# Softcap attention, gated MLP and cosine MLP on one core: the background conversion of the second MLP's weights moves beside the first MLP

## The chip, the core and the metric

One core of a Trainium2 chip runs the whole kernel as one program. Its engines run side by side, each through its own queue in order: TensorE (PE, matmuls; PEld its weight loads), VectorE (DVE), ScalarE (ACT), GpSimd (POOL) and SyncE (SP), which issues the DMAs here. They wait for each other by semaphores. The metric is the device time of one execution in microseconds (us).

## What is computed

Inputs are float32 and float64; the weights of the MLPs come as float64 and are converted to float32 on the chip.

```python
scores = cap * tanh((q @ k.T) / sqrt(64) / cap)       # batch 4, heads 12, seq 448, head_dim 64
attn   = softmax(scores) @ v                           # sum + 1e-9 in the denominator
x = attn.transpose(0, 2, 1, 3).reshape(1792, 768)
x = (sigmoid(x @ w_gate) * (x @ w_val)) @ w_out        # d_ff 1536
h = x @ w_in2                                          # d_ff 2048
return (h * cos(h)) @ w_out2                           # 1792 x 768
```

## The kernel before

**Tiles and halves.** The 1792 tokens are worked in two halves of 896 (two batches of 448). A float32 product is made of three matmuls: each operand is split into a rounded part and a rest, and `mm3` (L496) adds rest x rounded and rounded x rest to rounded x rounded. A tile of weights, a *unit*, is 128 x 768 (some 128 x 512).

**Order of the stages.** Attention of half 0; the first MLP of half 0 with pieces of the attention of half 1 between; attention of half 1; the first MLP of half 1; the second MLP of half 1; the second MLP of half 0. The result y of the first MLP on half 0 waits in DRAM (`ykept`) and is fetched and split again by `y_again` (L579) in the last group of the second MLP of half 1; the tiles are then `yr` (fetched) and `ya` (split).

**First MLP** (`mlp1`, L514). Twelve rounds m: 36 matmuls of the gate (`pg`), 36 of the value (`pv`). ACT makes the sigmoid of `pg` (L545) beside `pv`, DVE multiplies (L547), ACT and DVE split the product (L549, L550). Then six y rounds of 72 matmuls (`py`); ACT copies y out of PSUM (L574), DVE makes its rest (L575). `pg`, `pv`, `py` and later `ph` take turns in the two buffers of one PSUM pool (`psS`, L93), so the next `pg` needs the sigmoid of this one, and `py` of round m+2 the y copy of round m.

**Second MLP** (`mlp2`, L594). f-groups of 6, 5 and 5 tiles. Per f tile 36 matmuls `ph` (L500), then a chain of ACT and DVE for h cos h (`hidden`, L659), with a split that gives z; then the products `po` of the group (L619), which ACT copies or DVE adds into `acc`.

**Weights.** A unit that is there in float32 is fetched from DRAM (`f<-kept`, L140), rounded by ACT (L224), and its rest is made by POOL (L225). Three are fetched ahead; the tiles f have four slots (`FB`, L64), shared with the background's tiles `fb`.

**Background** (`background`, L196). The second MLP's weights, 34 units, are converted in three steps each, in program order between other work; each `next(others)` is one step:

```python
        for _ in signs(raw[u], g):            # step 1: ACT: Abs (L156) into fb, Sign (L158)
        ...                                   #         and the DMA of the next raw unit
        next(c); next(c)                      # step 2: DVE L163, L165
        for _ in c: pass                      # step 3: DVE L169, L173
        nc.sync.dma_start(out=kept[u][:, : nk * n], in_=g)   # write-back, L214
```

One further step in front loads the first raw unit: 103 steps. Before, 4 steps follow each of the twelve gate/value rounds (`PIECES`), 4 lie in each y round (`BESIDE_Y`), 2 follow each `hidden` of the second MLP of half 1 (`PIECES_H`), and some lie between its products (`BESIDE_O`).

The order on each engine is the order of the program (`manual_schedule`, L715): nothing is moved ahead of what was written first.

Of the kernel before, what the change touches and what calls it, by code (L numbers as in the profile page):

```python
# [27 lines left out]
def softcap_attention_gated_mlp_cos_mlp(  # L28
# [18 lines left out]
    nc = tc.nc  # L47
# [6 lines left out]
    KD, KF, KF2 = DM // P, DFF // P, DFF2 // P  # L54
    BH = 2
    TOK = BH * S
    NTT = TOK // P
# [11 lines left out]
    BESIDE = ((2, 10), (3, 2), (3, 6), (4, 1), (4, 5), (4, 8), (5, 1), (5, 5), (5, 8))  # L69

    PIECES, BESIDE_Y, PIECES_H, BESIDE_O = 4, (2, 5, 8, 11), 2, (4, 8, 12, 16, 20)

    AGAIN = (4, 6, 8, 10, 12, 14, 16)


    PVS = ((), (), (0, 1, 2, 3), ())
# [17 lines left out]
    def big_tile(shape, dtype, name):  # L96
        return big.tile(shape, dtype, tag="big", name=name)
# [27 lines left out]
    ykept = [dram.tile([P, BH, S], F32, tag=f"ykept{i}", name=f"ykept{i}") for i in range(KD)]  # L125
# [126 lines left out]
    def w_early():  # L252

        for _ in w_signs():
            pass

    def w_front(mid=nothing):

        if pos["conv"] == len(units):
            mid()  # L260
            return
        if pos["sign"] == pos["conv"]:
            w_early()
        for i, _ in enumerate(w_conv()):
            if i == 1:
                mid()
        w_loads()
# [6 lines left out]
    def w_back():  # L274
        if pos["split"] < len(units):
            if pos["keep"] == pos["split"]:
                w_keep()
            w_split()
            w_loads()
# [22 lines left out]
    def w_take():  # L302
        i = pos["use"]
        pos["use"] += 1
        return w_t.pop(i)
# [205 lines left out]
    def tmp_tile(name):  # L511
        return tmp.tile([P, BH, S], F32, tag="tmp", name=name)
# [66 lines left out]
    def y_again(y):  # L579

        raw = {}
        for m in range(-1, KD):
            if m + 1 < KD:
                raw[m + 1] = tmp_tile(f"yr{m + 1}")
                nc.sync.dma_start(out=raw[m + 1], in_=ykept[m + 1])
            if m >= 0:
                t = raw.pop(m)
                yt = big_tile([P, 2, BH, S], F32R, f"ya_{m}")
                nc.scalar.copy(out=yt[:, 0], in_=t)
                nc.vector.tensor_tensor(out=yt[:, 1], in0=t, in1=yt[:, 0].bitcast(F32), op=ALU.subtract)  # L590
                y.append(yt)
            yield

    def mlp2(hf, y, others, beside):  # L594
        acc = {}
        for gi, (f0, nf) in enumerate(groups):
            last = gi == len(groups) - 1
            z = []
            for f in range(f0, f0 + nf):
                t, more = hidden(hf, f, y, f0 + nf - 1 - f)  # L600
                z.append(t)
                for _ in range(PIECES_H):
                    next(others, None)
            zf = [t.rearrange("p a c s -> p a (c s)") for t in z]
            for nb in range(DM // NB):
                ws = [w_take() for _ in range(0, nf, UK)]
                pos_t = {}

                def out_tile(t, name):
                    if nb == 0 and t == EARLY - 1:  # L610
                        return more[:, 0]
                    return psA.tile([P, 512], F32, tag="A", name=name)

                def product(t, kks):
                    for kk in kks:
                        if kk == 0:
                            pos_t[t] = out_tile(t, f"po{hf}_{gi}_{nb}_{t}")
                        for zi, wi in ((0, 0), (0, 1), (1, 0)):
                            nc.tensor.matmul(  # L619
                                pos_t[t][:, :NB],  # L620
                                lhsT=zf[kk][:, zi, t * P : (t + 1) * P],
                                rhs=ws[kk // UK][:, wi, kk % UK, :],
                                start=(kk == 0 and (zi, wi) == (0, 0)),
                                stop=(kk == nf - 1 and (zi, wi) == (1, 0)),
                            )


                early = range(EARLY if nb == 0 else 0)
                for t in range(NTT):
                    if t == 0:  # L630
                        for e in early:
                            product(e, range(nf - 2))
                        for e in early:
                            product(e, range(nf - 2, nf - 1))
                    product(t, range(nf - 1 if t in early else 0, nf))
                    ps = pos_t.pop(t)
                    if gi == 0:
                        if t == 0:
                            acc[nb] = big_tile([P, NTT, NB], F32, f"acc{hf}_{nb}")
                        nc.scalar.copy(out=acc[nb][:, t], in_=ps[:, :NB])  # L640
                    else:
                        a = acc[nb][:, t]
                        nc.vector.tensor_tensor(out=a, in0=ps[:, :NB], in1=a, op=ALU.add)
                    if t == 2:
                        w_back()
                    if t in ((0, 2, 4) if nb == 0 else (0, 3)):
                        w_early()
                    if t in ((2, 4, 6) if nb == 0 else (2, 5)):
                        w_front()
                    if t == NTT - 1:  # L650
                        w_back()
                    if last:
                        store(hf, t, nb, acc[nb][:, t])
                        if nb * NTT + t in AGAIN:
                            next(beside, None)
                    elif nb * NTT + t in BESIDE_O:
                        next(others, None)

    def hidden(hf, f, y, left):  # L659

        w = w_take()
        ps = ps_tile(f"ph{hf}_{f}")
        more = ps_tile(f"more{hf}_{f}") if left == 0 else None
        for kk in range(KD):
            mm3(ps, w, kk, y[kk], kk == 0, kk == KD - 1)

        h = tmp_tile(f"h{hf}_{f}")
        u = tmp_tile(f"u{hf}_{f}")
        n = tmp_tile(f"n{hf}_{f}")
        zt = big_tile([P, 2, BH, S], F32R, f"z{hf}_{f}")  # L670

        def fraction(c):
            nc.scalar.activation(out=u[:, c], in_=ps[:, c, :S], func=AF.Identity, scale=INV_TWO_PI, bias=quarter)  # L673
            nc.vector.tensor_scalar_add(out=n[:, c], in0=u[:, c], scalar1=ROUND)  # L674
            nc.vector.scalar_tensor_tensor(
                out=u[:, c], in0=n[:, c], scalar=ROUND, in1=u[:, c], op0=ALU.subtract, op1=ALU.subtract
            )

        def product(c, h):
            nc.scalar.activation(out=u[:, c], in_=u[:, c], func=AF.Sin, scale=-TWO_PI_LOW)  # L680
            nc.vector.tensor_tensor(out=n[:, c], in0=h, in1=u[:, c], op=ALU.mult)

        def split(c, engine):
            nc.scalar.copy(out=zt[:, 0, c], in_=n[:, c])
            engine.tensor_tensor(out=zt[:, 1, c], in0=n[:, c], in1=zt[:, 0, c].bitcast(F32), op=ALU.subtract)

        both = slice(0, BH)
        if left == 0:
            for c in range(BH):
                fraction(c)  # L690
            for c in range(BH):
                product(c, ps[:, c, :S])
                split(c, nc.vector)
            w_back()
        else:
            nc.scalar.copy(out=h, in_=ps[:, :, :S])
            fraction(both)
            w_step(lambda: product(both, h))
            split(both, nc.vector if left == 1 else nc.gpsimd)
        return zt, more  # L700
# [14 lines left out]
    with tc.manual_schedule():  # L715
        nc.vector.memset(zeros, 0.0)
        nc.vector.reciprocal(out=tanh_scale, in_=cap_sb)
        nc.vector.tensor_scalar_mul(out=tanh_scale, in0=tanh_scale, scalar1=1.0 / float(D) ** 0.5)
        nc.scalar.activation(out=guard, in_=cap_sb, func=AF.Exp, scale=-1.0)
        nc.vector.tensor_scalar_mul(out=guard, in0=guard, scalar1=1e-9 / CP)  # L720
        att = [attention(hf) for hf in range(B // BH)]
        steps = 3 + (BH * NP + 1) * NC - LAST
        for _ in range(steps):
            next(att[0])
        mlp1(0, att[0], att[1])
        for _ in range(steps - len(BESIDE)):
            next(att[1])
        others = background()
        y = mlp1(1, att[1], others)
        y_first = []  # L730
        mlp2(1, y, others, y_again(y_first))
        mlp2(0, y_first, iter(()), iter(()))


# [33 lines left out]
```

## Time and profile before

| | |
|---|---|
| median of 3 runs | 1275.12 us (1274.87 to 1278.29) |
| profiled execution | 1271.98 us, span 1270.2 us, mean granted clock 0.985 |
| busy share of the span | PE 96%, PEld 83%, DVE 55%, ACT 47%, POOL 35% |
| the chain that ended last | PE 72%, DVE 13%, ACT 6%, issue 4%, DMA 3% |

The chain is followed back from the last instruction to what released each step. Times in timelines are us from the start of the span; a figure in brackets is the time that the engine stood idle before the row, and what released it. `x36` is the number of instructions merged in a row.

### The profile page before, as it was taken

The page shows a single profiled execution, that of the slowest core. Times are in us where ns is not written, and L with a number is a line of the kernel's source. Part 1 is how long each engine was busy: PE and PEld are TensorE (multiplying, and loading weights), DVE is VectorE, ACT ScalarE, POOL GpSimd, SP SyncE. Part 2 cuts the span into 40 slices and gives each one's busy share as a digit, 9 for nine tenths or more (in the row PEclk, how much of TensorE's full clock was granted, in tenths as well). Part 3 has the DMA queues.
Part 4 walks back from the last instruction along what each step waited for, and adds up shares of the span by engine and source line. Part 5 has one row for each costly group of instructions (what it writes and reads, how often), then busy time and mean ns, then how long its engine had stood idle before and what let it go on. Part 6 is the DMA issues. An engine that isn't in the chain of part 4 may idle for free.

```text
span 1270.2 us, 17272 instructions
## 1 busy us (share of the span) xinstructions
PE 1220.0 (96%) x7014; PEld 1051.7 (83%) x7014; DVE 696.4 (55%) x757; ACT 593.5 (47%) x678; POOL 449.9 (35%) x234
## 2 busy tenths in 40 slices
PE   8989999999999999999999997699699999999998
PEld 4445889999985558899999996699599999999998
DVE  6998797778516983455445445514543435024252
ACT  7885654445337892433343335435414335344150
POOL 3766232233216672232223233223233234335041
PEclk9999999999999999999999999899799999999999
DMA  6422465446633313455455523332231441213012
GB/s 154 138 72 87 150 211 188 160 150 223 189 108 99 88 30 102 131 165 173 147 168 163 182 87 100 112 104 83 91 104 34 138 146 50 63 42 97 8 47 83
DMA packets 131376, 148.26 MB, mean 117 GB/s; under 512 B 50529, under 2 KB 101345, under 8 KB 131297
## 3 DMA queue, kind: packets, MB, share of 16 engines
q1 hardware_dynamic: 131008, 147.09, 38.0%
q8 instruction: 55, 0.90, 0.3%
q14 instruction: 25, 0.20, 0.1%
q10 hardware_dynamic: 288, 0.07, 0.0%
HBM read 112.13 MB, written 35.00 MB: 116 GB/s over the span
## 4 chain that ended last, share of the span: by engine, by line
PE 72%; DVE 13%; ACT 6%; issue 4%; DMA 3%; POOL 1%; SPq 1%; DVEq 0%; ACTq 0%; POOLq 0%
PE po L619 16%; PE ph L500 13%; PE py L500 12%; PE pv L500 11%; PE pg L500 10%; PE pv L408 4%; PE s L379 3%; DMA kept<-fb 2%; DVE r L427 1%; PE t L358 1%; DVE fb L169 1%; DVE fb L173 1%; ACT p L382 1%; DVE f L169 1%; PE den L424 1%
## 5 line engine op out<-in xcount | busy, mean ns | idle before, releaser
L225 POOL TENSOR_TENSOR w<-f,w 128x768 fp32r<-128x768 f32 (+1 forms) x140 | 271.3, 1943 | 704.0 <-ACT w L224 572.9
L619 PE MATMUL po<-w,z 128*128 128x256 f32 x1920 | 243.3, 288 | 21.6 <-ACT w L224 7.8
L619 PEld LDWEIGHTS po<-w,z 128*128 128x128 f32 x1920 | 239.0, 196 | 24.6 <-ACT w L224 8.0
L500 PE MATMUL pv<-x,w 128*128 128x448 f32 x864 | 180.7, 366 | 1.2 <-DVE sg L547 1.2
L500 PE MATMUL pg<-x,w 128*128 128x448 f32 x864 | 180.8, 367 | 0.1
L500 PE MATMUL py<-g,w 128*128 128x448 f32 x864 | 179.1, 367 | 0.5 <-ACT sg L545 0.5
L500 PEld LDWEIGHTS pv<-x,w 128*128 128x128 f32 x864 | 161.9, 188 | 17.0 <-issue 3.3
L500 PEld LDWEIGHTS pg<-x,w 128*128 128x128 f32 x864 | 161.8, 188 | 16.2 <-ACT sg L545 1.1
L500 PEld LDWEIGHTS py<-g,w 128*128 128x128 f32 x864 | 161.5, 188 | 16.1 <-issue 1.0
L500 PE MATMUL ph<-y,w 128*128 128x448 f32 x576 | 121.0, 372 | 7.4 <-ACT u L673 7.4
L224 ACT CAST w<-f 128x768 fp32r<-128x768 f32 (+1 forms) x140 | 111.8, 808 | 30.1 <-DVE f L173 16.2
L500 PEld LDWEIGHTS ph<-y,w 128*128 128x128 f32 x576 | 110.2, 192 | 17.4 <-ACT u L673 8.2
L674 DVE TENSOR_SCALAR n<-u 128x896 f32<-128x896 f32 (+1 forms) x38 | 26.2, 690 | 172.5 <-ACT u L673 172.5
L500 PE MATMUL ph<-ya,w 128*128 128x448 f32 x576 | 117.2, 365 | 0.0
L500 PEld LDWEIGHTS ph<-ya,w 128*128 128x128 f32 x576 | 108.0, 188 | 8.5
L382 ACT ACTIVATE p<-s,tanh_scale 112x896 f32<-112x896 f32 x96 | 93.1, 1011 | 43.3 <-PE s L379 43.2
L388 ACT ACTIVATE p<-p,cap_sb 112x1792 f32<-112x1792 f32 x48 | 86.4, 1799 | 0.1
L379 PEld LDWEIGHTS s<-st 64*112 64x112 f32 x576 | 46.4, 174 | 41.0 <-ACT p L382 19.0
L408 PE MATMUL pv<-p,v 112*64 112x448 f32 x384 | 77.5, 545 | 2.0 <-PE t L358 2.0
L379 PE MATMUL s<-st 64*112 64x448 f32 x576 | 74.4, 385 | 1.6 <-ACT p L382 1.4
L427 DVE RECIPROCAL r<-den 128x448 f32<-128x448 f32 x24 | 70.8, 2950 | 8.6 <-PE den L424 8.6
L163 DVE TENSOR_SCALAR fb<-fb 128x768 f32<-128x768 f32 (+1 forms) x34 | 30.0, 882 | 82.6 <-ACT fb L156 82.6
(82 smaller groups left out, 1237.9 us busy)
## 6 DMA issues: line engine op xcount, KB each, us to landing
f<-kept SPq DMA_DIRECT2D x92, 384.0 KB, 3.1
kept<-f SPq DMA_DIRECT2D x36, 384.0 KB, 2.7
wi_raw<-in_moe_w_in_dram SPq DMA_DIRECT2D x16, 768.0 KB, 5.1
kept<-fb SPq DMA_DIRECT2D x28, 384.0 KB, 2.7
wg_raw<-in_moe_w_gate_dram SPq DMA_DIRECT2D x12, 768.0 KB, 5.1
wv_raw<-in_moe_w_val_dram SPq DMA_DIRECT2D x12, 768.0 KB, 4.7
wo_raw<-in_moe_w_out_dram SPq DMA_DIRECT2D x12, 768.0 KB, 4.8
wz_raw<-in_moe_w_out_dram SPq DMA_DIRECT2D x12, 768.0 KB, 4.9
```

Of the source, the lines that this page charges most:

```text
L163: nc.vector.tensor_scalar(out=g, in0=g, scalar1=F64_MIN_HI, scalar2=F64_MAX_HI, op0=ALU.max, op1=ALU.min)
L169: nc.vector.scalar_tensor_tensor(out=gi, in0=lo, scalar=28, in1=gi, op0=ALU.logical_shift_right, op1=ALU.bitwise_or)
L224: nc.scalar.copy(out=t[:, 0], in_=r)
L225: nc.gpsimd.tensor_tensor(out=t[:, 1], in0=r, in1=t[:, 0].bitcast(F32), op=ALU.subtract)
L379: nc.tensor.matmul(ps[:CP, h, :S], lhsT=st[r, ki, ks], rhs=st[r, qi], start=(n == 0), stop=(n == 2))
L382: nc.scalar.activation(out=pt[:CP, j], in_=ps[:CP, :, :S], func=AF.Tanh, scale=tanh_scale[:CP])
L388: nc.scalar.activation(out=pt[:CP], in_=pt[:CP], func=AF.Exp, scale=cap_sb[:CP])
L408: nc.tensor.matmul(pv[h * D : (h + 1) * D, :S], lhsT=tv[:, h, c, :], rhs=pt[:CP, j, h, :], start=(c == 0), stop=(c == NC - 1),)
L427: nc.vector.reciprocal(out=r[:, 0], in_=den[:, :S])
L500: nc.tensor.matmul(ps[:, c, :S], lhsT=w[:, wi, kk, :], rhs=x[:, xi, c, :], start=(first and (wi, xi) == (0, 0)), stop=(last and (wi, xi) = ...
L619: nc.tensor.matmul(pos_t[t][:, :NB], lhsT=zf[kk][:, zi, t * P : (t + 1) * P], rhs=ws[kk // UK][:, wi, kk % UK, :], start=(kk == 0 and (zi, ...
L674: nc.vector.tensor_scalar_add(out=n[:, c], in0=u[:, c], scalar1=ROUND)
```

## The change

The steps of the background lie beside the first MLP of half 1 alone: 5 behind each gate/value round, 7 in each y round; what is left is issued behind the y rounds. The second MLP no longer has steps of it. `y_again` issues a fetch two of its steps ahead of the conversion, before one, and begins at product 2 instead of 4.

```diff
-    PIECES, BESIDE_Y, PIECES_H, BESIDE_O = 4, (2, 5, 8, 11), 2, (4, 8, 12, 16, 20)
-
-    AGAIN = (4, 6, 8, 10, 12, 14, 16)
+    PIECES, BESIDE_Y = 5, (0, 2, 4, 6, 8, 9, 11)
+
+    AGAIN = (2, 4, 6, 8, 10, 12, 14, 16)
@@ def y_again(y):
-        for m in range(-1, KD):
-            if m + 1 < KD:
-                raw[m + 1] = tmp_tile(f"yr{m + 1}")
-                nc.sync.dma_start(out=raw[m + 1], in_=ykept[m + 1])
+        for m in range(-2, KD):
+            if m + 2 < KD:
+                raw[m + 2] = tmp_tile(f"yr{m + 2}")
+                nc.sync.dma_start(out=raw[m + 2], in_=ykept[m + 2])
@@ def mlp2(hf, y, beside):
                 z.append(t)
-                for _ in range(PIECES_H):
-                    next(others, None)
...
                         if nb * NTT + t in AGAIN:
                             next(beside, None)
-                    elif nb * NTT + t in BESIDE_O:
-                        next(others, None)
@@ main
         y = mlp1(1, att[1], others)
         y_first = []
-        mlp2(1, y, others, y_again(y_first))
-        mlp2(0, y_first, iter(()), iter(()))
+        for _ in others:
+            pass
+        mlp2(1, y, y_again(y_first))
+        mlp2(0, y_first, iter(()))
```

The lines of the changed kernel have numbers one less than before up to the last part (L155 is L156, L223 is L224).

ACT's order before, gate/value round 3 of half 1: from the split of its product (`g_3`) to the sigmoid of round 4 (`sg_4`); `fb` is a unit of the background.

```order
L549 CAST g_3_4408<-sg_3_4363 128x896
L224 CAST w_4411<-f_4266 128x768
L156 ACTIVATE fb_4419<-wi_raw 128x768
L158 ACTIVATE wi_raw<-wi_raw,tiny 128x768
L545 ACTIVATE sg_4_4466<-pg_4_4429 128x896
```

The same place in the changed kernel:

```order
L548 CAST g_3_4418<-sg_3_4373 128x896
L223 CAST w_4421<-f_4271 128x768
L155 ACTIVATE fb_4429<-wi_raw 128x768
L157 ACTIVATE wi_raw<-wi_raw,tiny 128x768
L155 ACTIVATE fb_4439<-wz_0_0_raw 128x768
L157 ACTIVATE wz_0_0_raw<-wz_0_0_raw,tiny 128x768
L544 ACTIVATE sg_4_4481<-pg_4_4444 128x896
```

A second Abs and its Sign stand ahead of the sigmoid of round 4.

ACT's order before, from the last y rounds into the second MLP of half 1 (`h_0`, `u_0` belong to its first f tile):

```order
L224 CAST w_5746<-f_5602 128x768
L574 CAST y_4_5751<-py_4_5653 128x896
L224 CAST w_5796<-f_5648 128x768
L156 ACTIVATE fb_5819<-wi_raw 128x768
L158 ACTIVATE wi_raw<-wi_raw,tiny 128x768
L224 CAST w_5844<-f_5700 128x768
L574 CAST y_5_5849<-py_5_5754 128x896
L696 COPY h_0_5889<-ph_0_5852 128x896
L673 ACTIVATE u_0_5890<-ph_0_5852,quarter 128x896
...
L684 CAST z_0_5892<-n_0_5891 128x896
L156 ACTIVATE fb_5909<-wi_raw 128x768
L158 ACTIVATE wi_raw<-wi_raw,tiny 128x768
```

The same place in the changed kernel:

```order
L573 CAST y_4_5841<-py_4_5733 128x896
L155 ACTIVATE fb_5880<-wz_2_0_raw 128x768
L157 ACTIVATE wz_2_0_raw<-wz_2_0_raw,tiny 128x768
L223 CAST w_5891<-f_5728 128x768
L155 ACTIVATE fb_5925<-wz_2_3_raw 128x512
L157 ACTIVATE wz_2_3_raw<-wz_2_3_raw,tiny 128x512
L223 CAST w_5942<-f_5783 128x768
L573 CAST y_5_5947<-py_5_5844 128x896
L691 COPY h_0_5990<-ph_0_5953 128x896
L668 ACTIVATE u_0_5991<-ph_0_5953,quarter 128x896
...
L679 CAST z_0_5993<-n_0_5992 128x896
L691 COPY h_1_6044<-ph_1_6007 128x896
```

The Abs of the 34th and last unit now stands ahead of the copy of y_5; no Abs follows in the second MLP.

## Rows read from the trace of the kernel before

**Rows 1.** By stretch: length, busy (xcount) PE PEld DVE ACT POOL, clock, DMA share, GB/s.

```profile
743.80:858.30 114.50, 96.18 (x595) 90.69 (x594) 50.55 (x47) 47.73 (x69) 31.45 (x15) 0.93 0.30 95
858.30:951.50 93.20, 80.30 (x498) 76.19 (x497) 46.02 (x61) 34.49 (x45) 28.93 (x15) 0.91 0.30 95
951.50:1028.30 76.80, 75.35 (x498) 71.86 (x497) 30.71 (x46) 31.26 (x39) 24.68 (x14) 1.00 0.36 107
1028.30:1117.50 89.20, 89.20 (x596) 85.90 (x595) 23.01 (x28) 37.06 (x57) 31.08 (x16) 1.00 0.23 66
1117.50:1191.80 74.30, 74.30 (x497) 71.63 (x496) 25.96 (x41) 27.01 (x35) 27.42 (x15) 1.00 0.19 57
1191.80:1266.30 74.50, 74.45 (x497) 71.57 (x495) 26.34 (x43) 23.41 (x30) 20.11 (x11) 1.00 0.19 53
```

**Rows 2.** Timeline of ACT, second MLP of half 1: start, length, instruction, idle before.

```profile
765.38 0.90 ACT L156 ACTIVATE fb<-wi_raw 128x768 f32<-128x768 f32 x1 [7.23 <-DMA kept<-fb]
...
767.18 0.89 ACT L696 COPY h<-ph 128x896 f32<-128x896 f32 x1
```

**Rows 3.** Timeline of PE, from the y rounds into the second MLP.

```profile
654.58 89.40 PE L500 MATMUL py<-g,w 128*128 128x448 f32 x432 [0.50 <-ACT sg L545]
743.82 22.48 PE L500 MATMUL ph<-y,w 128*128 128x448 f32 x108
769.03 14.86 PE L500 MATMUL ph<-y,w 128*128 128x448 f32 x72 [2.73 <-ACT u L673]
788.55 10.32 PE L500 MATMUL ph<-y,w 128*128 128x448 f32 x36 [4.66 <-ACT u L673]
```

**Rows 4.** Timeline of ACT, y rounds of the first MLP.

```profile
665.74 0.89 ACT L156 ACTIVATE fb<-wi_raw 128x768 f32<-128x768 f32 x1 [8.38 <-DMA kept<-fb]
...
672.74 0.90 ACT L156 ACTIVATE fb<-wi_raw 128x768 f32<-128x768 f32 x1 [5.06 <-DMA kept<-fb]
...
674.60 1.56 ACT L224 CAST w<-f 128x768 fp32r<-128x768 f32 x2
...
738.56 0.91 ACT L156 ACTIVATE fb<-wi_raw 128x768 f32<-128x768 f32 x1 [6.34 <-DMA kept<-fb]
```

**Rows 5.** Timeline of SP's queue: two write-backs of the background, issued.

```profile
594.60 0.32 SPq L214 DMA_DIRECT2D kept<-fb  x1
...
669.91 0.32 SPq L214 DMA_DIRECT2D kept<-fb  x1
```

**Rows 6.** Timeline of DVE, y rounds.

```profile
668.92 0.96 DVE L173 SCALAR_TENSOR_TENSOR fb<-fb,wi_raw 128x768 int32<-128x768 int32 x1
...
675.93 2.42 DVE L173 SCALAR_TENSOR_TENSOR fb<-fb,wi_raw 128x768 int32<-128x768 int32 x1
678.27 1.08 DVE L575 TENSOR_TENSOR y<-py,y 128x896 fp32r<-128x896 f32 x1
```

**Rows 7.** Chain of waits, last group of the second MLP, half 1.

```profile
1004.68 4.81 DMA yr<-ykept
```

**Rows 8.** Timeline of ACT, gate/value rounds.

```profile
590.43 0.90 ACT L156 ACTIVATE fb<-wz_raw 128x768 f32<-128x768 f32 x1 [6.73 <-DMA kept<-fb]
...
607.25 0.91 ACT L156 ACTIVATE fb<-wz_raw 128x768 f32<-128x768 f32 x1 [4.89 <-DMA kept<-fb]
...
609.08 0.91 ACT L545 ACTIVATE sg<-pg 128x896 f32<-128x896 f32 x1
```

**Rows 9.** Timeline of PE, gate/value rounds.

```profile
573.33 7.46 PE L500 MATMUL pv<-x,w 128*128 128x448 f32 x36
580.62 7.46 PE L500 MATMUL pg<-x,w 128*128 128x448 f32 x36
```

**Rows 10.** Busy time by stretch, behind the wait at 788.55; columns as in rows 1.

```profile
788.50:792.00 3.50, 3.45 (x9) 3.10 (x10) 2.42 (x3) 1.67 (x2) 0.00 (x0) 0.50 0.00 0
796.00:800.00 4.00, 3.95 (x24) 3.54 (x22) 1.70 (x1) 0.00 (x0) 0.88 (x1) 1.00 0.48 152
```

**Rows 11.** Costliest groups of the page: busy us, mean ns of one, idle before.

```profile
L225 POOL TENSOR_TENSOR w<-f,w 128x768 fp32r<-128x768 f32 (+1 forms) x140 | 271.3, 1943 | 704.0 <-ACT w L224 572.9
```

More of the change, by code (lines that the diff above doesn't have):

```diff
@@ L592, in y_again, with mlp2 @@
             yield
-    def mlp2(hf, y, others, beside):
+    def mlp2(hf, y, beside):
         acc = {}
```

## The prediction

> **What bounds the kernel now.** I read the table of stages first, then the timelines of PE, ACT, SP and DVE at the places the change touches. TensorE bounds the kernel: it is busy nearly throughout, except in two stretches [rows 1]. These are the first two f-groups of the second MLP on the second half of the tokens (743.8 to 951.5). The same code on the first half, later, takes 89.2 and 74.3 us with PE busy throughout; here it takes 114.5 and 93.2 us, with the granted clock at 0.93 and 0.91. The code differs in one thing: here the background conversion runs in between. What it does is seen on ACT [rows 2]: an Abs (L156) of the background waits 7.23 us for the write-back of the unit before it, and the copy of `ph` (L696), whose matmuls were over, comes only behind it. PE then waits, 4.66 us before one group of 36 matmuls [rows 3].
>
> So the background has a chain of its own: Abs on ACT, four operations on DVE, the write-back `kept`, and only then the next Abs, because the f loads hold the other three f slots. One unit alone takes 7.0 us, from 665.74 to 672.74 [rows 4]. Its write-back is issued at 669.91 [rows 5] and lands 2.8 us later. Over nine Abs, 665.74 to 738.56, the eight intervals mean 9.1 us [rows 4]. Between them lie eleven weight copies (L224), the first two at 674.60 [rows 4], each followed by a subtraction on POOL (L225). With one of these beside it the last DVE operation takes 2.42 instead of 0.96 us [rows 6]; f loads, y copies and y subtractions come between as well. Beside the first MLP this chain runs as it does in the second; but there PSUM's two buffers give ACT time, and PE hardly waits.
>
> **The change part by part.** The amount of conversion stays: 34 units, 103 steps. Before, 72 steps lay beside the first MLP and 31, some ten units, beside the second; now 60 lie in its twelve gate/value rounds (5 per round, before 4), 42 in the six y rounds (7, before 4), and the last is issued right behind them.
>
> *Removed from the second MLP.* The second half then runs the code that the first half runs. I take the first half's times: 114.5 + 93.2 - 89.2 - 74.3 = 44.2 us gained [rows 1], clock included. Of that little can be missing, since nothing else differs in those two groups. Lower bound: if only the ten Abs's own waits went but the other stalls stayed, perhaps half, 22.
>
> *Fetching y two steps ahead.* It adds no DMA. The six loads of 448 KB are issued one of its steps earlier, two output tiles, and so pass the stores of two tiles on SP's queue; the conversions stay where they were. In the last group the chain of waits goes twice through a `yr` load, the first time 4.81 us [rows 7]. The group takes 76.8 us against 74.5 for the first half's [rows 1]. At most 2.3 us go, at worst none; I take 2.0. What hides the earlier loads are the products of two more tiles; without that cover the 2.0 stay.
>
> *Gate/value rounds, 5 steps.* Let E be the end of `pv` of a round. Call a unit's steps s (Abs and Sign), a and b (the halves on DVE, b with the write-back). Of three rounds in a row the first reads s a b s a, the second b s a b s, the third a b s a b. The first kind is in the profile already, less its last a: second Abs at 607.25, sigmoid at 609.08, done at 609.98 [rows 8]; PE's next `pg` needs that buffer 14.6 us after E (two times 7.29, [rows 9]), so it just holds. The second kind was there only without its last s. There E is 580.79 [rows 9], the Abs starts at 590.43 [rows 8], its write-back is issued at 594.60 [rows 5], 13.8 behind E. The added Abs stands in ACT's order ahead of the next sigmoid: 13.8 + 2.8 landing + 2.73 (from that Abs's start to the sigmoid's end, 607.25 to 609.98) = 19.4 us behind E. PE waits 19.4 - 14.6 = 4.8 us. The third kind then catches up: its write-back lands before PE needs it. Such rounds are the rounds 3, 6 and 9 of 0 to 11: 3 x 4.8 = 14.4 us. Queued behind the waiting Abs are the sigmoid, the weight copy (L224) and with it POOL's subtraction; PE waits for the sigmoid first.
>
> *The clock.* After the 4.66 us wait the granted clock was 0.50, that is 1.2 of 2.4 GHz, and 1.00 again in the stretch from 796 [rows 10]; the 36 matmuls took 10.32 instead of 7.46 us [rows 3, 9]: 2.9 us. A wait of 4.8 us should do the same: 3 x 2.9 = 8.7. Bounds: 0 if the clock holds, 8.7.
>
> *The y rounds, 7 steps.* Steps run ahead of PE, since no step waits for it, so the background goes at its chain's pace, not PE's. PE gives 89.2 us for six rounds (654.58 to 743.82, [rows 3]); 14 units at 9.1 would need 127. My value for a unit: bare 7.0, the measured mean 9.1 with 11 weight copies on 8 intervals (1.4 a unit); now 12 on 14 (0.86), so 7.0 + 2.1 x 0.86/1.4 = 8.25 us, 14 x 8.25 = 115.5. The round before y is of the first kind, so its second Abs stands 11.8 us behind E (607.25 - 595.4, E one round of 14.6 behind 580.79). The last Abs is then at E + 127.3. Then come on ACT this Abs and its Sign (some 0.7 each at 512 columns, the 0.90 of [rows 4] scaled), a weight copy (0.78, half of the two of [rows 4]) and the copy of y_5 (0.89, as `ph`'s of the same size in [rows 2]), then y_5's subtraction on DVE (1.08, [rows 6]) and the last four matmuls of `ph` 0 (0.8), together 5.0 us: E + 132.3. Before, `ph` 0 ended at 743.82 + 7.46 = 751.3 and E was 654.58 - 0.50 = 654.1 [rows 3], so 97.2. Loss 35.1 us. What waits: `py` for the weight copy and the y copy that stand behind an Abs, in small pieces, then `ph` 0 for w, y_4 and y_5. One more loss of clock, 2.9, behind the longest wait; those inside the y rounds cost nothing, since ACT is later than PE there. Bounds for the loss: 14 units at 7.0 give 17.6, at 9.1 they give 47.
>
> A rule speaks against this size. The row shows that one collision with POOL costs DVE 1.46 us (2.42 - 0.96), and a subtraction takes 1.94 us on average [rows 11]. The Trainium skill, "SBUF — State Buffer", section "SBUF: two separate sides", says that DVE and GpSimd lock their shared port pair exclusively, for a whole instruction. By that rule a DVE operation that comes just behind a subtraction's start waits for nearly all of it. My 8.25 us hold 17.5 us of collisions and the like (14 x 1.25); a whole subtraction for each of the 12 copies would be 23.3.
>
> *Sum.* 14.4 + 8.7 + 35.1 + 2.9 = 61.1 lost, 44.2 + 2.0 = 46.2 gained: 14.9 us slower. The profiled execution took 1271.98 us (span 1270.2), so 1286.9; the median of the three runs, 1275.12, lies 3.1 above it, so I predict 1290.
>
> **The rivals.**
> *The other side: the chain is quick.* If nothing collides in the y rounds and the units of 512 columns, 4 of the 14, are shorter (by a third in the operations, so some 5.4 us by estimate), they take 10 x 7.0 + 4 x 5.4 = 91.6 instead of 115.5: 9.0 us faster than before, 1266. It decides at 8.25 - 14.9/14 = 7.2 us a unit. For it: the first of the eight intervals is 7.0. Against it: their mean. Chance 0.12.
> *The clock holds*, because the waits come out a little shorter than 4.66: 11.6 less, 3.3 slower, 1278. For it: behind a wait of 2.73 us 72 matmuls took 14.86 us, full speed [rows 3]. Chance 0.13.
> *Every collision costs the most it can.* A whole subtraction for each of the 12 copies makes 14 x 7.0 + 23.3 = 121.3, 5.8 more, 1296; units that stay at the mean of 9.1 make 127.4, 11.9 more, 1302. For it: the mean of the eight intervals, and more traffic than before. Against it: fewer copies per unit. Chance 0.17.
> *The second MLP keeps half of its stalls*: 22 less gained, 1312. Against it: the first half's time. Chance 0.03.
>
> **How the numbers follow.** My forecast has 0.55; its own range is 1281 to 1298. About 0.3%, 3.8 us, is what this measurement can tell. Faster by more: nearly all of the first rival, 0.11. Within: most of the second and little of the rest, 0.11. Slower: 0.78. The range of 1270 to 1304 leaves out most of the first rival and all of the fourth, 0.13, and little of the rest.
>
> **What would show it.** Right: the two groups from the first `ph` on take 89 and 74 us at clock 1.00; three gaps of nearly 5 us ahead of `pg` in rounds 5, 8 and 11, released by the sigmoid, with slow matmuls behind; the y rounds and `ph` 0 take some 35 us more, with `ph` 0 held by y_5, and ACT's idle time there ended by `kept`. Wrong: Abs intervals below 7.2 us in the y rounds, or a first sigmoid gap that is missing; then the whole is faster. If gaps remain in the second MLP, the gain was not the background's.

## The result and the profile after

The changed kernel takes 1290.54 us (median of 4 runs, 1288.03 to 1291.71) against 1274.99 (1270.05 to 1278.29) for the kernel before: ratio 1.0134, 95% interval 1.01 to 1.0168. It is 15.5 us slower; predicted were 14.9 us, and a time of 1290. Its profiled execution has a span of 1288.6 us, 18.4 more than before. Followed along PE, the difference comes from these stretches (us):

| stretch | before | after | difference | predicted |
|---|---|---|---|---|
| start to the first `pg` of half 1 (472.24, 475.79) | 472.2 | 475.8 | +3.6 | 0 |
| gate/value rounds of half 1, to the first `py` | 182.3 | 205.0 | +22.6 | +23.1 |
| y rounds and `ph` 0, to ACT's copy of `ph` 0 | 96.9 | 134.2 | +37.4 | +35.1 |
| rest of f-groups 1 and 2 | 200.0 | 157.6 | -42.5 | -44.2 + 2.9 |
| f-group 3 | 76.8 | 74.3 | -2.5 | -2.0 |
| half 0 of the second MLP and the end | 241.9 | 241.7 | -0.2 | 0 |

The first line is no work of the change: the code there is the same (the last section comes back to it). Without it the rows sum to 14.8.

The table of stages of the changed kernel; columns as in [rows 1].

```profile
680.80:813.60 132.80, 105.22 (x466) 94.05 (x465) 63.05 (x71) 42.79 (x52) 25.30 (x14) 0.89 0.50 159
813.60:898.30 84.70, 84.70 (x563) 81.66 (x563) 21.64 (x26) 38.45 (x58) 29.52 (x15) 0.97 0.21 65
898.30:972.60 74.30, 74.30 (x498) 71.62 (x497) 25.90 (x41) 27.02 (x35) 27.37 (x15) 1.00 0.20 57
972.60:1046.90 74.30, 74.30 (x498) 71.62 (x497) 31.73 (x48) 31.26 (x39) 26.34 (x14) 1.00 0.38 113
```

Two things are to be seen. Behind `ph` 0 PE is busy throughout the second MLP now: where [rows 1] had 93.2 and 76.8 us there are 74.3 twice. And the y rounds with `ph` 0, in which PE hardly waited before, now leave it idle for 27.6 us (132.80 - 105.22). What PE waited for from the first MLP of half 1 on: us in total, times, longest.

```profile
PE pg L499 <- ACT sg L544: 17.4, 6, 5.1
PE py L499 <- DVE y L574: 14.8, 4, 5.4
PE ph L499 <- ACT y L573: 10.4, 1, 10.4
PE ph L499 <- DVE y L574: 2.4, 1, 2.4
```

The longest two of the kernel before, over the same stretch, were these:

```profile
PE po L619 <- ACT w L224: 7.8, 1, 7.8
PE ph L500 <- ACT u L673: 7.4, 2, 4.7
```

Both lay in the second MLP and are gone, like its smaller ones; what stands in the list now is the sigmoid's and the y copies'. PE's timeline has them at the places that were forecast; the rows answer to [rows 3] and [rows 9].

```profile
511.74 7.56 PE L499 MATMUL pg<-x,w 128*128 128x448 f32 x36 [1.84 <-ACT sg L544]
...
561.60 9.50 PE L499 MATMUL pg<-x,w 128*128 128x448 f32 x36 [5.06 <-ACT sg L544]
...
612.86 9.57 PE L499 MATMUL pg<-x,w 128*128 128x448 f32 x36 [4.86 <-ACT sg L544]
...
664.52 9.13 PE L499 MATMUL pg<-x,w 128*128 128x448 f32 x36 [4.98 <-ACT sg L544]
673.48 7.46 PE L499 MATMUL pv<-x,w 128*128 128x448 f32 x36
680.77 29.35 PE L499 MATMUL py<-g,w 128*128 128x448 f32 x144
...
795.11 6.46 PE L499 MATMUL ph<-y,w 128*128 128x448 f32 x30 [2.35 <-DVE y L574]
811.99 41.11 PE L499 MATMUL ph<-y,w 128*128 128x448 f32 x186 [10.42 <-ACT y L573]
```

The three gaps of 4.9 to 5.1 us stand ahead of `pg` of rounds 5, 8 and 11, and the 36 matmuls behind each take 9.1 to 9.6 us. `ph` 0 stops after 30 of 36 matmuls and waits 10.42 us for the copy of y_5.

ACT shows why. Round 3 of the gate/value rounds, which answers to [rows 8]: two Abs, the second behind a write-back, and only then the sigmoid, done at 561.55, just before PE starts at 561.60.

```profile
551.98 0.89 ACT L155 ACTIVATE fb<-wi_raw 128x768 f32<-128x768 f32 x1 [7.52 <-issue]
...
558.85 0.89 ACT L155 ACTIVATE fb<-wz_raw 128x768 f32<-128x768 f32 x1 [4.93 <-DMA kept<-fb]
...
560.65 0.90 ACT L544 ACTIVATE sg<-pg 128x896 f32<-128x896 f32 x1
```

And in the y rounds, which answer to [rows 4], ACT does little and waits for write-backs to the end; the copy of y_5 (L573) comes behind the last Abs.

```profile
685.98 0.66 ACT L155 ACTIVATE fb<-wz_raw 128x512 f32<-128x512 f32 x1 [2.13 <-POOL w L224]
...
691.39 0.89 ACT L155 ACTIVATE fb<-wz_raw 128x768 f32<-128x768 f32 x1 [3.94 <-DMA kept<-fb]
...
808.97 0.66 ACT L155 ACTIVATE fb<-wz_raw 128x512 f32<-128x512 f32 x1 [6.64 <-DMA kept<-fb]
...
811.04 0.90 ACT L573 CAST y<-py 128x896 fp32r<-128x896 f32 x1
```

From the Abs at 691.39 to the one at 808.97 are 14 units in 117.6 us, 8.40 each.

### The profile page after: what moved, and what is told of

It is laid out like the page before. It is cut to its first block, busy times and chain, and to the rows that moved or that the text cites. A ratio compares the mean times of both kernels' runs of the same rounds, so it can differ in the third digit from the quotient of the medians.

```text
span 1288.6 us, 17313 instructions
## 1 busy us (share of the span) xinstructions
PE 1226.7 (95%) x7014; PEld 1055.2 (82%) x7014; DVE 681.4 (53%) x757; ACT 595.1 (46%) x678; POOL 446.4 (35%) x234
## 4 chain that ended last, share of the span: by engine, by line
PE 66%; DVE 14%; ACT 6%; issue 6%; DMA 5%; POOL 2%; SPq 0%; ACTq 0%; DVEq 0%; POOLq 0%
PE ph L499 18%; PE po L616 18%; PE py L499 7%; PE pv L499 7%; PE pg L499 7%; DMA kept<-fb 5%; PE pv L407 3%; PE s L378 3%; DVE fb L172 3%; DVE fb L168 2%; ACT fb L155 2%; DVE r L426 1%; PE t L357 1%; ACT p L381 1%; DVE f L168 1%
## 5 line engine op out<-in xcount | busy, mean ns | idle before, releaser
L224 POOL TENSOR_TENSOR w<-f,w 128x768 fp32r<-128x768 f32 (+1 forms) x140 | 270.3, 1935 | 725.9 <-ACT w L223 647.4
L616 PE MATMUL po<-w,z 128*128 128x256 f32 x1920 | 234.4, 283 | 0.0
L616 PEld LDWEIGHTS po<-w,z 128*128 128x128 f32 x1920 | 232.6, 192 | 0.3
L499 PE MATMUL pg<-x,w 128*128 128x448 f32 x864 | 187.6, 376 | 17.4 <-ACT sg L544 17.4
L499 PE MATMUL py<-g,w 128*128 128x448 f32 x864 | 187.9, 379 | 14.8 <-DVE y L574 14.8
L499 PEld LDWEIGHTS pg<-x,w 128*128 128x128 f32 x864 | 166.1, 193 | 36.8 <-ACT sg L544 19.9
L499 PEld LDWEIGHTS py<-g,w 128*128 128x128 f32 x864 | 168.2, 196 | 32.2 <-DVE y L574 16.3
L223 ACT CAST w<-f 128x768 fp32r<-128x768 f32 (+1 forms) x140 | 112.0, 808 | 29.1 <-DVE f L172 16.1
L162 DVE TENSOR_SCALAR fb<-fb 128x768 f32<-128x768 f32 (+1 forms) x34 | 24.8, 728 | 102.2 <-ACT fb L155 102.2
```

Of the source, the lines that this page charges most:

```text
L223: nc.scalar.copy(out=t[:, 0], in_=r)
L224: nc.gpsimd.tensor_tensor(out=t[:, 1], in0=r, in1=t[:, 0].bitcast(F32), op=ALU.subtract)
L499: nc.tensor.matmul(ps[:, c, :S], lhsT=w[:, wi, kk, :], rhs=x[:, xi, c, :], start=(first and (wi, xi) == (0, 0)), stop=(last and (wi, xi) = ...
L616: nc.tensor.matmul(pos_t[t][:, :NB], lhsT=zf[kk][:, zi, t * P : (t + 1) * P], rhs=ws[kk // UK][:, wi, kk % UK, :], start=(kk == 0 and (zi, ...
```

## The experiments

Theory A is the prediction's: the background is a chain through one tile slot (the next Abs waits until the write-back of the last unit has landed), and since ACT works in order, what stands behind a waiting Abs is late. Theory B, the rival: the loss is the price of so much conversion beside the first MLP, its share of DVE, of the port with POOL and of the DMA engines, whatever the order or the slot.

**The same steps, three Abs moved behind a sigmoid.**

```diff
-                for _ in range(PIECES):
+                for _ in range(PIECES - (m in (3, 6, 9))):
                     next(beside, None)
@@ behind the sigmoid and w_step() of the gate part
+                        if hf and m in (4, 7, 10):
+                            next(beside, None)
```

> The changed kernel, but the fifth step of gate/value rounds 3, 6 and 9 of half 1 (an Abs and its Sign) is issued behind the next round's sigmoid instead of ahead of it. Same steps, same slot, same traffic. Theory A (the Abs that waits for a write-back stands ahead of the sigmoid): the three gaps of 4.9 us and the slow matmuls behind them (some 2.0 us each) go, 20.7 us, to about 1270; the y rounds stay as they are. Theory B (the loss is the amount of conversion, port and DMA traffic beside the first MLP): no change, about 1290.

Measured: 1273.85 us (median of 10), 1.0006 of the kernel before (0.9993 to 1.002), 16.7 us less than the changed kernel. (The two ran beside different runs of the kernel before; each taken against its own, 1272.89 here and 1274.99 there, the gain is 14.6.) What PE waited for:

```profile
PE py L499 <- DVE y L576: 15.5, 4, 5.6
PE ph L499 <- ACT y L575: 8.8, 1, 8.8
PE pg L499 <- ACT sg L544: 6.3, 5, 2.1
```

The waits for the sigmoid fall from 17.4 to 6.3 us, the longest from 5.1 to 2.1; those of the y rounds stay. The work is the same, so theory B has no account of it. The gain is 4 us or more short of the forecast: the trace has smaller gaps, of 0.7 to 1.3 us, ahead of four other rounds, and behind the one of 2.06 us ahead of round 2 the 36 matmuls take 9.16 us.

**The same steps, slots of their own.**

```diff
-            g = f_tile(f"b{u}")[:, : nk * n]
+            g = tmp.tile([P, UW], F32, tag="tmp", name=f"b{u}")[:, : nk * n]
```

> The changed kernel, but the background's tiles come from the pool of temporary tiles (four slots, one of them taken by the sigmoid's tile) instead of sharing the four f slots. Same steps at the same places, same bytes. Theory A (a chain through one slot: the next Abs waits until the write-back has landed): an Abs waits for its raw unit only, ACT keeps up, the gaps ahead of pg and in the y rounds go: 36 us of the y rounds and ph 0, 17 us of waits and some 6 of clock in the gate/value rounds, together up to 58, to about 1233. Theory B (amount of conversion and traffic beside the first MLP): at most a few us, 1285 or more.

Measured: 1226.18 us (median of 4, 1225.16 to 1230.29), 0.9632 of the kernel before (0.9604 to 0.9661): this version beats both kernels, by 48.8 us (46.7 against the kernel before on its own chip) and by 64.4. That is 6 us more than was expected; half of these are in the y rounds and `ph` 0, which give back 39 us and not 36. From the first MLP of half 1 on, PE waited for one thing only:

```profile
PE pg L499 <- ACT sg L544: 1.2, 3, 0.6
```

The stages, the y rounds first, then f-groups 1 and 2; columns as in [rows 1].

```profile
654.00:745.00 91.00, 91.00 (x451) 84.34 (x450) 64.48 (x71) 41.24 (x50) 23.46 (x13) 1.00 0.71 234
745.40:834.70 89.30, 89.30 (x596) 85.98 (x595) 24.20 (x27) 39.60 (x60) 31.32 (x16) 1.00 0.21 65
834.70:909.00 74.30, 74.30 (x497) 71.63 (x497) 25.89 (x41) 27.02 (x35) 27.41 (x15) 1.00 0.19 57
```

The same conversions lie in the y rounds as in the changed kernel, in 91 us instead of 133 (with `ph` 0), with DVE at 64.48 us, the DMA engines at 0.71 and 234 GB/s (0.50 and 159 above), and PE is busy in all of it. So neither DVE nor the port nor the traffic was the limit, and theory B falls. The run also gives the weights their fourth f slot back; no wait of PE in the changed kernel's list is for a weight. What an Abs on ACT waits for is now the load of its raw unit (us in total, times, longest):

```profile
ACT b L155 <- DMA wz_raw<-in_moe_w_out_dram: 42.3, 13, 7.5
ACT b L155 <- DMA wi_raw<-in_moe_w_in_dram: 34.1, 10, 7.6
```

In the changed kernel it was the write-back, 26 times, and longer:

```profile
ACT fb L155 <- DMA kept<-fb: 152.6, 26, 8.4
```

**The kernel before with slots of its own.**

```diff
-            g = f_tile(f"b{u}")[:, : nk * n]
+            g = (tmp.tile([P, UW], F32, tag="tmp", name=f"b{u}") if u - N1 < 23 else f_tile(f"b{u}"))[:, : nk * n]
```

> The kernel before, with its steps where they were, but the background's tiles of the units that begin beside the first MLP (23 of 34) come from the pool of temporary tiles; the later units keep the f slots. Theory A: beside the first MLP there was hardly a wait of PE to save, and in the second MLP the Abs still wait for a write-back ahead of the copies of ph, so its two groups take some 114 and 93 us: 1270 to 1274, as before; with that the placement alone is worth some 44 us once the slot is not shared (1226 against this run). Rival: the own slots are worth some 45 us wherever the steps lie; then about 1230.

Measured: 1273.61 us, one run, beside 1270.79 for the kernel before. The waits are still where the steps are, in the second MLP; its longest is 10.5 us, ahead of a `po`, and its first two f-groups take about as long as in [rows 1]:

```profile
743.75:859.90 116.15, 96.08 (x595) 90.77 (x594) 50.73 (x47) 47.74 (x69) 31.23 (x15) 0.91 0.28 90
859.90:953.20 93.30, 81.00 (x497) 76.83 (x496) 45.99 (x61) 34.47 (x45) 28.91 (x15) 0.91 0.29 95
```

So own slots beside the first MLP bring nothing by themselves, and the move by itself costs 15.5 us; both together bring 48.8. Against this run the move, with the earlier fetch of y, is worth 47 us; the prediction has 46.2 of gains. One rival stays untested: the units of the second MLP (and a 24th, which begins beside the first) kept the f slots here, so no run shows what slots of their own would bring there without the move.

**Five steps in the gate/value rounds, the rest as before.**

```diff
-    PIECES, BESIDE_Y, PIECES_H, BESIDE_O = 4, (2, 5, 8, 11), 2, (4, 8, 12, 16, 20)
+    PIECES, BESIDE_Y, PIECES_H, BESIDE_O = 5, (2, 5, 8, 11), 2, (4, 8, 12, 16, 20)
```

> The kernel before with 5 instead of 4 steps in each gate/value round; the y rounds keep 4, and 19 steps are left, 17 of them beside the first f-group of the second MLP and its products. Theory A: three gaps of some 5 us ahead of pg in rounds 5, 8 and 11 as in the changed kernel and their clock, together with the smaller waits some 22 us; y rounds as before; first f-group still some 114 us; second f-group 74 us instead of 93: in all about 1278. Theory B (a price per step): 12 of 31 steps, so 12/31 of the loss of 58, the same 22; here the two agree on the time and differ on the place: under B the loss is spread over all rounds.

Measured: 1275.19 us, one run, 2.3 above the 1272.89 of the kernel before on that chip. The gaps ahead of `pg` of rounds 5, 8 and 11, as in the changed kernel, the y rounds in one piece, and the first two f-groups:

```profile
557.83 9.46 PE L500 MATMUL pg<-x,w 128*128 128x448 f32 x36 [5.06 <-ACT sg L545]
...
608.95 9.59 PE L500 MATMUL pg<-x,w 128*128 128x448 f32 x36 [4.69 <-ACT sg L545]
...
660.71 9.12 PE L500 MATMUL pg<-x,w 128*128 128x448 f32 x36 [5.02 <-ACT sg L545]
...
676.97 87.71 PE L500 MATMUL py<-g,w 128*128 128x448 f32 x432
```

```profile
764.50:878.00 113.50, 97.88 (x595) 92.54 (x595) 49.18 (x47) 46.82 (x69) 32.62 (x16) 0.91 0.28 89
878.00:952.90 74.90, 74.74 (x498) 71.78 (x497) 31.88 (x45) 28.12 (x37) 27.46 (x15) 1.00 0.21 66
```

Nearly all of the loss stands in the three rounds (14.8 of the 16.9 us that PE waited for the sigmoid), not spread over twelve. The gain comes group by group: the second f-group, with two steps left in it, takes 74.9 us, the first, with 17, takes 113.5.

**Seven steps in the y rounds, the rest as before.**

```diff
-    PIECES, BESIDE_Y, PIECES_H, BESIDE_O = 4, (2, 5, 8, 11), 2, (4, 8, 12, 16, 20)
+    PIECES, BESIDE_Y, PIECES_H, BESIDE_O = 4, (0, 2, 4, 6, 8, 9, 11), 2, (4, 8, 12, 16, 20)
```

> The kernel before with 7 instead of 4 steps in each y round; the gate/value rounds keep 4, and 13 steps are left, 12 of them behind the hidden tiles of the first f-group. Theory A (one slot, one chain): y rounds and the first f tile some 36 us longer, the last Abs of the y rounds holding the copy of y_5; first f-group still some 114 us, second 74 to 75 instead of 93; no new gap ahead of pg: in all about 1290. Theory B (a price per step): 18 of 31 steps, so 34 us on, and the gain of the second f-group off: about 1288. The place tells: under A the loss is in the y rounds' waits and at y_5.

Measured: 1293.37 us, one run, 22.6 above the 1270.79 of the kernel before on that chip; 3 more than expected. No large gap ahead of `pg`; the y rounds and `ph` 0 are as in the changed kernel, and the first f-group has its waits still, while the second, which has no steps left, takes 74.3 us (899.10 to 973.40):

```profile
PE py L500 <- DVE y L575: 14.3, 4, 5.7
PE ph L500 <- ACT y L574: 9.9, 1, 9.9
PE po L619 <- ACT w L224: 6.6, 1, 6.6
```

**y fetched one step ahead again.**

```diff
-    AGAIN = (2, 4, 6, 8, 10, 12, 14, 16)
+    AGAIN = (4, 6, 8, 10, 12, 14, 16)
@@ y_again
-        for m in range(-2, KD):
-            if m + 2 < KD:
+        for m in range(-1, KD):
+            if m + 1 < KD:
...
```

> The changed kernel with y fetched one step ahead again, from product 4, as before. Theory: the last group of the second MLP on half 1 takes 76.8 us again instead of 74.3, all else as in the changed kernel: about 1293. Rival: the group takes 74.3 without the earlier fetch too, since the chain arrives there undisturbed; then 1290.

Measured: 1292.15 us, one run; its time alone tells nothing about an effect of this size. The group's own time does:

```profile
971.70:1048.60 76.90, 75.51 (x497) 71.83 (x496) 31.09 (x47) 31.27 (x39) 25.10 (x14) 1.00 0.35 107
```

76.9 us, as before, instead of 74.3, and PE waits ahead of `po` again (four times, 1.3 us in all). The earlier fetch is worth 2.6 us.

## Why the prediction was right, step by step

*What bounds the kernel.* Right: the second MLP's waits went with the steps; f-groups 2 and 3 take the 74.3 us of the other half's code. The 157.6 us of the table hold what was left of the slow clock behind the wait at 811.99. The earlier fetch of y is worth 2.6 us, more than the 2.3 that were called the most.

*Gate/value rounds.* The three gaps were forecast at 4.8 us each ahead of rounds 5, 8 and 11; they measure 5.06, 4.86 and 4.98. Moving the three Abs took them away, which shows the cause and does not only fit it. Two terms inside the sum were off and cancel. The clock's price was put at 2.9 us per gap from one row and measures 1.7 to 2.0, 5.7 instead of 8.7 us in all (9.50, 9.57 and 9.13 us against 7.46 and, at the slower pace, 7.60). And gaps of 2.5 us in all were not seen, 1.84 of them ahead of round 2: round 0 has an Abs as its fifth step too. Its first Abs waited 4.02 us for the first raw unit, the second 5.06 us for the write-back, and the sigmoid of round 1 stands behind both.

*The clock.* It fell as forecast behind each of the three gaps; the stretch behind the first of them, columns as in [rows 1]:

```profile
561.60:566.00 4.40, 4.40 (x12) 3.94 (x13) 3.40 (x3) 2.34 (x3) 3.33 (x2) 0.52 0.15 47
566.00:571.00 5.00, 5.00 (x27) 4.63 (x26) 3.71 (x4) 0.00 (x0) 0.82 (x1) 1.00 0.42 143
```

*The y rounds.* The mechanism is right, and that the slot is the cause, not the load, is shown by the run with own slots. The size is in part luck. 8.25 us a unit were forecast (the formula itself gives 8.29) and 8.40 measured, but the formula starts from 7.0 for every unit, and four of the 14 have 512 columns; one of these alone takes 5.41 us (685.98 to 691.39). By the bare times of both sizes the 14 units would take 91.6 us, so what came on top is 26.0 us, not the 17.5 of the forecast. The mean of 9.1 from which the forecast started had three such short units among its eight, so it came out nearly right. The chain began 10.5 us behind E (691.39 - 680.94), not 11.8, since the unit ahead has 512 columns. From the last Abs to ACT's copy of `ph` 0 went 6.05 us instead of 5.0, the last six matmuls at a granted clock of 0.50.

*The rule on the shared port.* The Trainium skill, "SBUF — State Buffer", section "SBUF: two separate sides", says that of a GpSimd operation and a DVE operation with two inputs in SBUF the one that starts first holds their shared port pair for its whole instruction. The trace agrees, operation by operation:

```profile
709.32 1.96 POOL L224 TENSOR_TENSOR w<-f,w 128x768 fp32r<-128x768 f32 x1 [6.94 <-ACT w L223]
```

```profile
709.72 2.38 DVE L172 SCALAR_TENSOR_TENSOR fb<-fb,wz_raw 128x768 int32<-128x768 int32 x1
```

The DVE operation takes 0.96 us alone ([rows 6]); here it starts when 1.56 us of the subtraction are left and takes 1.42 longer. Eleven subtractions of POOL lie in the 14 units. Eight meet this operation so, each time with what was left of the subtraction less 0.14 to 0.15 us: 1.41 to 1.55 us each, 11.8 in all. The other three run beside a subtraction of y (L574), which has one input in PSUM and keeps its 1.09 us. So the rival's whole subtraction per copy, 23.3 us, did not come, because not every copy collides and a collision costs what is left of the subtraction. The rest of the 26.0 us is in the main 8.9 in three units whose DVE operations stood behind a subtraction of y, and four write-backs that took 3.5 to 4.9 us where an undisturbed one takes 2.6.

*The rivals.* The quick chain (7.2 us a unit or less) did not come, the clock did not hold, and the second MLP kept none of its stalls.

*The total.* That 1290 and 1290.54 agree to half a microsecond is luck: 3.6 us of the difference between the two profiled executions come from the first line of the table, which no term of the sum had, and the runs of the kernel before lie 8 us apart.

## What to carry to other kernels

Work that is laid beside an idle engine can be bound by a chain of its own: look at what ends the engine's idle time, and if it is the write-back of the work's own last tile, compute the length of that chain, not its busy time. In an in-order queue every instruction behind such a wait is late by it, so lay waiting work behind, not ahead of, what PE needs next. Give background tiles their own slots before moving them; the same move cost 1.3% with one slot and gained 3.7% with several.

## What was not expected of the hardware

TensorE has two paces at a granted clock of 1.00, in the same code. In the first MLP of half 0, groups of 36 matmuls start 7.29 us apart in the kernel before and 7.44 in the changed one, though nothing differs there.

```profile
175.53 7.46 PE L500 MATMUL pg<-x,w 128*128 128x448 f32 x36
182.82 7.46 PE L500 MATMUL pv<-x,w 128*128 128x448 f32 x36
```

```profile
175.88 7.60 PE L499 MATMUL pg<-x,w 128*128 128x448 f32 x36
183.32 7.60 PE L499 MATMUL pv<-x,w 128*128 128x448 f32 x36
```

Over that MLP it makes 3.4 of the 3.6 us of the table's first line. Within one execution the pace was seen to change only where PE had paused, as at 511.74 above. What decides it stays open. It may be part of the 8 us by which the runs of the kernel before differ; no run shows that.

The length of a wait alone does not tell whether the clock falls. At the same place of the same code, the second MLP of half 1, PE waited 2.73 us in the kernel before and in the run of that kernel with own slots. The matmuls behind it take 14.86 us in the one ([rows 3]) and 16.42 in the other:

```profile
768.97 16.42 PE L500 MATMUL ph<-y,w 128*128 128x448 f32 x72 [2.73 <-ACT u L673]
```

The five microseconds behind the wait, first in the kernel before, then in the run with own slots; columns as in [rows 1]:

```profile
769.00:774.00 5.00, 4.97 (x24) 4.62 (x25) 3.94 (x4) 2.77 (x4) 1.45 (x1) 1.00 0.00 0
```

```profile
769.00:774.00 5.00, 5.00 (x17) 4.50 (x18) 3.95 (x4) 2.83 (x4) 1.46 (x1) 0.66 0.00 0
```

So the second rival's ground, that the clock had held behind a wait of 2.73 us, was one case of two; and in the run with own slots the next wait, of 3.12 us, was followed by 36 matmuls at full speed (7.57 us).
